# Gated linear attention and a GELU MLP on one core: deeper load buffers, three slots for xT, and more transposes by the DMA crossbar

## The chip, the core and the metric

The kernel runs on one core of one Trainium2 chip. The metric is the device time of one execution in microseconds (us). A core has five engines with instruction streams of their own that meet only at semaphores: TensorE (PE; its weight loads are a row of their own, PEld), VectorE (DVE), ScalarE (ACT), GpSimd (POOL) and SyncE (SP). Sixteen DMA engines move data; here SP and POOL start the transfers.

## What is computed

The first half is a gated recurrent attention over 4 batches, 8 heads, 768 tokens and heads of 48; the second is a two-layer MLP with GELU over all 3072 tokens.

```python
state = zeros((B, H, D, D))                       # B 4, H 8, S 768, D 48
for t in range(S):
    state = alpha[:, :, t, :, None] * state + einsum('bhd,bhe->bhde', k[:, :, t], v[:, :, t])
    y[:, :, t] = einsum('bhd,bhde->bhe', q[:, :, t], state)
x = y.transpose(0, 2, 1, 3).reshape(B * S, H * D)  # 3072 x 384
h = x @ w_in                                       # 384 -> 2048
g = 0.5 * h * (1.0 + tanh(c * (h + 0.044715 * h**3)))
return g @ w_out                                   # 2048 -> 384
```

Inputs and output are float32; the kernel computes in bf16 and f16 with float32 sums.

## The kernel before

**Units and pairs.** The 768 tokens are cut into six chunks `c` of 128. A unit is one chunk of one batch; a *pair* is a chunk of two batches. There are twelve pairs, numbered `m` from 0 to 11: pair 6 and pair 7 are the two pairs of chunk 3, pairs 8 and 9 those of chunk 4, pairs 10 and 11 those of chunk 5. "The seventh pair" is thus pair 6, and "the eighth" pair 7. The two units of a pair are called j = 0 and j = 1 here.

**The steps of one pair.** Loads of alpha (tile `a`), `q`, `k` and v (`vb`) by POOL's DMA queue (L243); the logarithm of alpha on ACT (L296, tile `la`); its running sum as a matmul with a triangle (L313 to L317, tile `cum`); two exponentials on ACT, `b` and `binv` (L342); q' = q * b and k' = k / b on DVE (L353, tiles `qp` and `kp`); both transposed (tile `qkT`); `at` = k' q' for each head on PE (L424, 16 matmuls for the pair); the causal mask on DVE (L431, tile `atm`, four operations); `kv` for the state (L441), which DVE carries on (L463, L466); `y` from the state and from `atm` (L478, L481); `x`, its bf16 copy by ACT or DVE (L488); x transposed (tile `xT`); then the MLP of the pair: 48 matmuls of layer 1 (L507, into `hT`, in eight groups of six), GELU on ACT (L513, eight), and layer 2 (L526, 16 matmuls for each unit into `acc`), the copy `ot` (L538) and the store by SP (L544).

**Two ways to transpose.** On PE, q' and k' of a pair take 16 transposes into PSUM (`turn`, L363) and copies out of it (`turned`, L381); x of a unit takes three transposes (`turn_x`, L495) and one copy by DVE (L499). By the crossbar, SP issues one DMA transpose for q' and one for k' of a pair (`turn_dma`, L401), and one for x of each unit (`turn_x_dma`, L407), straight from SBUF to SBUF. `TURN_QK` and `TURN_X` (L151) list the pairs that go by the crossbar. The DMA queue of SP carries the stores too, in the order in which the program issues them.

**What sets the order.** A list scheduler (`Scheduler.order`, L50) runs when the kernel is built. Each step is a `Task` with a cost for its engine, a priority and what it depends on; buffers are rings with a number of slots (`BUFS`, L158), and a task that takes a slot waits until the users of the slot's last content are done. Loads count as landing one after another. A transpose by the crossbar counts as landed after `W["landed"]`, and later by `late_x` where the caller gives it (L689: `late=W["late_x"] * (m < 7)`). The costs only decide the order; the instructions then run in that order on each engine and wait on the chip for what they need. An instruction of PE that waits keeps all behind it waiting.

**Buffers that the change touches.** `a`, `q`, `k` have 4 slots each, float32 v of the first two pairs (tile `v`) has 2, and bf16 `vb` has 6. `xT` has one tile for each of the six chunks (L194).

Of the kernel before, what the change touches and what calls it, by code (L numbers as in the profile page):

```python
# [5 lines left out]
BF16 = mybir.dt.bfloat16  # L6
F16 = mybir.dt.float16
F32 = mybir.dt.float32
# [128 lines left out]
class _Kernel:  # L137
# [10 lines left out]
             ('a', 1, 0, 1), ('a', 1, 1, 2), ('q', 1, 0, 1), ('k', 1, 0, 1), ('q', 1, 1, 2), ('k', 1, 1, 2))  # L148
    NARROW = (0, 1)

    TURN_QK, TURN_X = (8, 9, 10, 11), (7, 8, 9, 10, 11)  # L151

    EV_ACT = (0, 1, 2, 3)

# [1 line left out]

    URGENT = (2,)
    BUFS = dict(ca=1, yk=2, ff=4, la=3, qp=4, kp=4, b8=2, kn=2, qkT=4, atm=6, x=3, ot=5, bend=3, ends=8,  # L158
                a=4, q=4, k=4, v=2, vb=6)

    def __init__(self, ctx, tc, q, k, v, alpha, w_in, w_out, out):
        nc = self.nc = tc.nc
        self.tc, self.out = tc, out
        B, H, S, D = q.shape
        self.B, self.H, self.S, self.D = B, H, S, D
        C = self.C = 128
        self.NCH = S // C
        self.src = {"a": alpha, "q": q, "k": k, "v": v}
        self.w_in_dram, self.w_out_dram = w_in, w_out
        self.d_model, self.d_ff = w_in.shape  # L170
        self.NKT, self.NFT = self.d_model // C, self.d_ff // C

        self.const = ctx.enter_context(tc.tile_pool(name="const", bufs=1))
        self.sb = ctx.enter_context(tc.tile_pool(name="sb", bufs=1))
        self.ps = ctx.enter_context(tc.tile_pool(name="ps", bufs=1, space=bass.MemoryType.PSUM))

        const = self.const
        self.ut_h = const.tile([C, C], F16, name="ut_h")
        self.ut = const.tile([C, C], BF16, name="ut")
        self.gate = const.tile([C, 1], F32, name="gate")  # L180
        self.ut_blk = [const.tile([C, C], F16, name=f"ut_blk{i}") for i in range(2)]
        self.blk = const.tile([C, 4], F16, name="blk")
        self.ident = const.tile([C, C], BF16, name="ident")
        self.ones = const.tile([C, 1], F16, name="ones")
        self.zero = const.tile([C, 512], BF16, name="zero")
        self.w_in = [const.tile([C, self.NKT, self.d_ff // 4], BF16, name=f"w_in{i}") for i in range(4)]
        self.w_out = const.tile([C, self.NFT, self.d_model], BF16, name="w_out")
        self.half = const.tile([C, 2], F32, name="half")
        self.state = [[const.tile([C, H // 2, 2 * D], BF16, name=f"st{b}_{i}") for i in range(2)]
                      for b in range(B)]  # L190
        self.ring = {n: [const.tile([C, 2, H, 64], F16 if n == "la" else BF16, name=f"{n}{i}")
                         for i in range(self.BUFS[n])] for n in ("la", "qp", "kp")}
        self.used = {n: 0 for n in self.ring}
        self.xT = [const.tile([C, self.NKT, B, C], BF16, name=f"xT{c}") for c in range(self.NCH)]  # L194
        self.NG = 2
        self.gT = [const.tile([C, self.NFT, B * C], BF16, name=f"gT{i}") for i in range(self.NG)]
        self.eng = {"ACT": nc.scalar, "DVE": nc.vector}
# [30 lines left out]
    def load(self, n, c, i, lo=0, hi=2):  # L228

        nc, C, H, D, R = self.nc, self.C, self.H, self.D, self.R  # L230
        u = self.p[c, i]

        def emit(e):
            t = "vb" if n == "v" and u["m"] not in self.NARROW else n
            if t not in u:
                u[t] = self.tile(t, [C, 2, H, D], BF16 if t == "vb" else F32)
            dma = (nc.sync if e == "SP" else nc.gpsimd).dma_start
            src = self.src[n][2 * i + lo:2 * i + hi]
            if u["packed"] and n != "v":
                dma(u[n][:, lo].rearrange("p (o r) d -> p o (r d)", o=2),  # L240
                    src[0, :, c * C:(c + 1) * C].rearrange("h (g r) d -> g h (r d)", r=R))
            else:
                dma(u[t][:, lo:hi].rearrange("t b h d -> t (b h) d"), src.rearrange("b h s d -> s (b h) d")[c * C:(c + 1) * C])  # L243
        return emit
# [159 lines left out]
        return emit  # L404

    def turn_x_dma(self, u, i, c, b):
        return lambda e: self.nc.sync.dma_start_transpose(self.xT[c][:, :, b, :], u["x", i])  # L407

    def attn(self, u, units, apart):
        nc, H, C = self.nc, self.H, self.C  # L410
# [85 lines left out]
        return emit  # L496

    def turned_x(self, u, i, c, b):
        return lambda e: self.copy(e)(self.xT[c][:, :, b, :], u["xT_ps", i])  # L499

    def layer1(self, f, c, lo, hi, nt):
        def emit(e):
            w_in = self.w_in[nt // 4].rearrange("k j (c r) -> k j r c", r=self.NFT // 4)
            h = f["h", c, lo, nt] = self.tile("ff", [self.C, 2, (hi - lo) * self.C], F32, "hT")
            for s in range(2):
                for j in range(self.NKT):
                    self.nc.tensor.matmul(h[:, s], w_in[:, j, nt % 4 + s],  # L507
                                          self.xT[c][:, j, lo:hi].rearrange("p g t -> p (g t)"),
                                          start=j == 0, stop=j == self.NKT - 1, skip_group_check=True)
        return emit  # L510

# [35 lines left out]
    def tasks(self):  # L547
        s = self.s = Scheduler(self.BUFS, self.fill, 60000)
        B, NCH = self.B, self.NCH
# [5 lines left out]
        loads, n, gate, held = {}, 0, [], {}  # L555
# [26 lines left out]
        for step in self.LOADS:  # L582
            if step[0] == "v":
                rows(int(step[1:]), "v")
            elif step[:4] == "gate":
                r, m, j = step[4:].split()
                m, j = int(m), int(j)
# [11 lines left out]
        for m, (c, i) in enumerate(pairs):  # L599
            u, P = self.p[c, i], 100 * m  # L600
# [4 lines left out]
            for lo, hi in self.parts(m):  # L605
# [3 lines left out]
                x = [s.add(e, {"ACT": W[e] if e == "bend" else W["exp"] * n // 2}, P + 2 + j, self.exp(u, e, lo, hi), [cum], LN_EXP)  # L609
                     for j, e in enumerate(("b", "binv", "bend") if u["sums"] else ("b", "binv"))]  # L610
# [35 lines left out]
            vin = [loads["v", m, j] for j in range(2)]  # L646
# [4 lines left out]
            for j in range(2):  # L651
                o, k = P + 10 + 3 * j, kp[j]
# [27 lines left out]
            for j in range(2):  # L680
                b, o, k, ms, turned = 2 * i + j, P + 10 + 3 * j, kp[j], masks[j], turns[j]
                at = ats[m][-1 if m not in self.SINGLE else j]
                if m in self.NARROW:
                    vin[j].deps += turned
                y = s.add("y", {"PE": W["intra"] + (W["inter"] if c else 0)}, P + 20 + j, self.y(u, j, c, b),
                          ms + turned + [vin[j]] + ([states[b, c - 1]] if c else []))
                xc = s.add("x", {"ACT": W["xc_act"], "DVE": W["xc"]}, P + 20 + j, self.x(u, j), [y])
                if m in self.TURN_X:
                    xe = tx = s.add("turn", {"SP": W["turn"]}, P + 22 + j, self.turn_x_dma(u, j, c, b), [xc], xbar=W["xbar_x"], late=W["late_x"] * (m < 7))  # L689
                else:  # L690
                    tx = s.add("tx", {"PE": W["tx"]}, P + 22 + j, self.turn_x(u, j), [xc])
                    xe = s.add("xe", {"DVE": W["xe"]}, P + 22 + j, self.turned_x(u, j, c, b), [tx])
                    tx.take("yk", xe)
                y.take("yk", xc)
                xc.take("x", tx)
                users += [at, y]
                ms[0].take("atm", y)
                xts[c, b], ys[b, c] = xe, y
                vs.append(y)
                if c < NCH - 1:  # L700
                    if u["packed"]:
                        tb = s.add("t", {"PE": W["t4"]}, P + 29 + j, self.turn_back(u, j), turned)
                        k = s.add("ev", {"DVE": W["ev4"], "ACT": W["ev4_act"]}, P + 29 + j, self.turned_back(u, j), [tb])
                        tb.take("yk", k)
                        users.append(tb)
                        backs.append(tb)
                    kv = s.add("kv", {"PE": W["kv"]}, P + 30 + j, self.kv(u, j), [k, vin[j]])
                    st = states[b, c] = s.add("st", {"DVE": W["st" if c else "st0"]}, P + 30 + j, self.carry(u, j, c, b),
                                              [kv, end] + ([states[b, c - 1], ys[b, c - 1]] if c else []))
                    kv.take("yk", st)  # L710
                    vs.append(kv)
                    kvs.append(kv)
                    cs.append(st)
# [9 lines left out]
            qp[0].take("qp", *tq)  # L723
            kp[0].take("kp", *tq, *kvs)
            if m in self.NARROW:
                loads["v", m, 0].take("v", *vin)
                vin[0].take("vb", *vs)
            else:
                loads["v", m, 0].take("vb", *vs)
# [6 lines left out]
        f, gs, l2s, ots, parts_of, firsts = {}, {}, {}, [], [], []  # L736
# [108 lines left out]
```

## Time and profile before

| what | value |
|---|---|
| median of the runs | 181.47 us (181.79, 180.89, 183.69, 181.16) |
| the profiled execution | 181.33 us |
| its span in the profile | 179.6 us |
| granted TensorE clock | 1.00 |
| busy: DVE / ACT / POOL | 96.8 / 130.9 / 57.8 us |
| DMA moved | 28.14 MB, mean 157 GB/s |
| crossbar transposes | 10 of x, 4 of q', 4 of k' |
| chain that ended last, by engine | PE 90%, DMA 5%, ACT 1%, DVE 1% |

The profile is one execution, taken by the hardware profiler; times in it run from the span's start. A timeline line gives the start, the length, the engine, the line of the kernel, the operation with output<-input, the shape and the number of instructions merged. A row of a table by stretches gives the stretch, its length, then the busy time of PE, PEld, DVE, ACT and POOL with the number of instructions in brackets, the granted clock, the mean share of the DMA engines (above 1 when packets queue on an engine) and GB/s. A DMA row ends with the median time from issue to landing.

### The profile page before, as it was taken

What the parts mean: (1) busy time and instruction counts of PE and PEld (TensorE: products, weight loads), DVE (VectorE), ACT (ScalarE), POOL (GpSimd) and SP (SyncE); (2) the same over time, 40 slices, a digit from 0 to 9 for tenths busy, and PEclk for the clock granted to TensorE, in tenths of its full rate; (3) what the DMA queues carried; (4) which work ended last, traced back from release to release, by engine and by line L of the source; (5) the groups of instructions that cost most, each with busy time, mean ns of one, the idle gap of its engine ahead of it and who ended that gap; (6) DMA issues with size and microseconds to landing.
All of it is one profiled execution on the core that took longest, in us unless ns stands there. A gap on an engine that the chain in (4) does not pass through costs nothing.

```text
span 179.6 us, 4459 instructions
## 1 busy us (share of the span) xinstructions
PE 173.1 (96%) x1860; PEld 136.7 (76%) x1860; DVE 96.8 (54%) x191; ACT 130.9 (73%) x216; POOL 57.8 (32%) x64
## 2 busy tenths in 40 slices
PE   6979999999999999999999999999999999999993
PEld 2557699566896897798698779689688697796972
DVE  6579750145968795597499798199245415000000
ACT  4669778974898678858888757887987984491831
POOL 2396447984647766722721300000000000000000
PEclk9999999999999999999999999999999999999999
DMA  4999999999999999998992626552361270311102
GB/s 126 270 275 198 209 241 238 240 214 206 223 306 189 223 252 206 197 261 197 181 248 67 169 98 108 102 131 55 68 161 47 61 183 10 90 41 47 44 0 88
DMA packets 45956, 28.14 MB, mean 157 GB/s; under 512 B 34544, under 2 KB 42352, under 8 KB 45936
## 3 DMA queue, kind: packets, MB, share of 16 engines
q0 software_dynamic: 26464, 17.70, 59.1%
q1 hardware_dynamic: 19472, 10.16, 21.4%
q8 instruction: 14, 0.23, 0.6%
q14 instruction: 6, 0.05, 0.1%
HBM read 25.17 MB, written 4.72 MB: 166 GB/s over the span
## 4 chain that ended last, share of the span: by engine, by line
PE 90%; DMA 5%; ACT 1%; DVE 1%; SPq 0%; issue 0%; POOL 0%
PE hT L507 35%; PE acc L526 35%; PE at L424 4%; DMA v<-in_v_dram 3%; PE qkT_ps L363 3%; PE yps L481 3%; PE kv L441 2%; PE cum L313 2%; PE yps L478 2%; DMA a<-in_alpha_dram 2%; PE xT_ps L495 1%; PE idle L224 1%; PE cum L281 1%; PE cum L315 1%; PE k_ps L389 1%; ACT vb L324 1%
## 5 line engine op out<-in xcount | busy, mean ns | idle before, releaser
L507 PE MATMUL hT<-xT,w_in 128*128 128x256 bf16 x576 | 69.2, 273 | 0.0
L526 PE MATMUL acc<-w_out,gT 128*128 128x384 bf16 (+1 forms) x400 | 69.1, 319 | 0.0
L513 ACT ACTIVATE gT<-hT 128x512 bf16<-128x512 f32 x96 | 56.7, 597 | 16.5 <-PE hT L507 12.9
L507 PEld LDWEIGHTS <-w_in 128*128 128x128 bf16 x576 | 61.0, 113 | 1.2
L526 PEld LDWEIGHTS <-gT 128*128 128x128 bf16 x400 | 36.7, 97 | 19.2
L431 DVE TENSOR_TENSOR atm<-at,ut 128x512 bf16<-128x512 f32 x48 | 30.3, 683 | 13.2 <-PE at L424 13.1
L353 DVE TENSOR_TENSOR qp<-q,b 128x768 bf16<-128x768 f32 (+1 forms) x15 | 11.9, 794 | 25.3 <-ACT b L342 25.3
L538 ACT COPY ot<-acc 128x384 f32<-128x384 f32 (+1 forms) x18 | 8.3, 458 | 14.1 <-PE acc L526 11.9
L243 POOL DMA_DIRECT2D q<-in_q_dram x11 | 12.2, 1110 | 15.5 <-DVE xT L499 7.4
L243 POOL DMA_DIRECT2D vb<-in_v_dram x11 | 12.1, 1102 | 10.6 <-PE xT_ps L495 6.1
L243 POOL DMA_DIRECT2D k<-in_k_dram x11 | 12.2, 1107 | 4.9 <-DMA a<-in_alpha_dram 1.8
L243 POOL DMA_DIRECT2D a<-in_alpha_dram x11 | 12.2, 1114 | 4.5 <-DMA w_in<-in_moe_w_in_dram 1.4
L342 ACT ACTIVATE b<-cum 128x768 bf16<-128x768 f32 (+1 forms) x15 | 10.3, 683 | 3.9 <-PE cum L315 2.5
L215 ACT ACT_TABLE_LOAD x9 | 11.5, 1283 | 0.9 <-PEq L829 0.7
L353 DVE TENSOR_TENSOR kp<-k,binv 128x768 bf16<-128x768 f32 (+1 forms) x15 | 11.9, 791 | 0.0
L513 ACT ACT_TABLE_LOAD x9 | 11.5, 1283 | 0.2
L342 ACT ACTIVATE binv<-cum 128x768 bf16<-128x768 f32 (+1 forms) x15 | 10.2, 680 | 0.0
L381 DVE COPY qkT<-qkT_ps 128x1024 bf16<-128x1024 bf16 (+1 forms) x13 | 8.6, 686 | 2.7 <-PE qkT_ps L363 2.6
L488 DVE CAST x<-yps 128x384 bf16<-128x384 f32 x11 | 6.1, 558 | 7.0 <-PE yps L481 6.9
L224 PE MATMUL idle<-zero 128*128 128x512 bf16 x26 | 8.5, 436 | 1.2 <-DVE half L798 1.2
L463 DVE TENSOR_TENSOR stmp<-kv,st 128x384 f32<-128x384 f32 x16 | 8.8, 552 | 1.2 <-PE kv L441 1.2
L488 ACT CAST x<-yps 128x384 bf16<-128x384 f32 x13 | 6.2, 475 | 4.4 <-PE yps L481 4.4
(63 smaller groups left out, 165.8 us busy)
## 6 DMA issues: line engine op xcount, KB each, us to landing
out_dram<-ot SPq DMA_DIRECT2D x23, 192.0 KB, 2.3
a<-in_alpha_dram POOLq DMA_DIRECT2D x9, 384.0 KB, 11.4
q<-in_q_dram POOLq DMA_DIRECT2D x9, 384.0 KB, 11.2
k<-in_k_dram POOLq DMA_DIRECT2D x9, 384.0 KB, 11.3
vb<-in_v_dram POOLq DMA_DIRECT2D x9, 192.0 KB, 11.2
w_in<-in_moe_w_in_dram POOLq DMA_DIRECT2D x4, 384.0 KB, 9.6
w_out<-in_moe_w_out_dram POOLq DMA_DIRECT2D x4, 384.0 KB, 11.2
a<-in_alpha_dram SPq DMA_DIRECT2D x4, 192.0 KB, 4.0
```

Of the source, the lines that this page charges most:

```text
L215: nc.scalar.add_instruction(mybir.InstLoadActFuncSet(name=nc.get_next_instruction_name(), act_func_set_id=i, engine=mybir.EngineType.Activ ...
L224: self.nc.tensor.matmul(ps, self.zero[:, 0:self.C], self.zero, start=True, stop=True)
L243: dma(u[t][:, lo:hi].rearrange("t b h d -> t (b h) d"), src.rearrange("b h s d -> s (b h) d")[c * C:(c + 1) * C])
L342: self.nc.scalar.activation(u[n].rearrange("t i h d -> t i (h d)")[:, lo:hi], cum, AF.Exp, scale=1.0 if n == "b" else -1.0)
L353: self.nc.vector.tensor_tensor(out, rows, b, op=ALU.mult)
L381: self.copy(e)(t, ps)
L431: self.nc.vector.tensor_tensor(u["atm", i][:, o], u["at", i][o], self.ut[:, None, :].to_broadcast([self.C, self.H // 2, self.C]), op=ALU.mult)
L463: nc.vector.tensor_tensor(s, acc, old, op=ALU.add)
L488: self.copy(e)(x, u["y", i].rearrange("t h d -> t (h d)"))
L507: self.nc.tensor.matmul(h[:, s], w_in[:, j, nt % 4 + s], self.xT[c][:, j, lo:hi].rearrange("p g t -> p (g t)"), start=j == 0, stop=j == se ...
L513: return lambda e: self.nc.scalar.activation(self.gT[c % self.NG][:, nt:nt + 2, lo * self.C:hi * self.C], f.pop(("h", c, lo, nt)), AF.Gelu ...
L526: self.nc.tensor.matmul(f["acc", c, b][:, lo:hi], self.gT[c % self.NG][:, nt, b * self.C:(b + 1) * self.C], self.w_out[:, nt, lo:hi], star ...
```

## The change

Pair 7 is added to the pairs whose q' and k' are transposed by the crossbar, and pair 6 to those whose x is; `late_x` is counted for pairs below 6 instead of below 7. `a` gets 6 slots, `q` and `k` 5; the float32 v of pairs 0 and 1 takes slots of the ring of `a` and its own ring goes. `xT` has three tiles, which the chunks use in turn.

```diff
-    TURN_QK, TURN_X = (8, 9, 10, 11), (7, 8, 9, 10, 11)
+    TURN_QK, TURN_X = (7, 8, 9, 10, 11), (6, 7, 8, 9, 10, 11)
...
-                a=4, q=4, k=4, v=2, vb=6)
+                a=6, q=5, k=5, vb=6)
...
-        self.xT = [const.tile([C, self.NKT, B, C], BF16, name=f"xT{c}") for c in range(self.NCH)]
+        self.NX = 3
+        self.xT = [const.tile([C, self.NKT, B, C], BF16, name=f"xT{c}") for c in range(self.NX)]
...
-                u[t] = self.tile(t, [C, 2, H, D], BF16 if t == "vb" else F32)
+                u[t] = self.tile("a" if t == "v" else t, [C, 2, H, D], BF16 if t == "vb" else F32, t)
...
-        return lambda e: self.nc.sync.dma_start_transpose(self.xT[c][:, :, b, :], u["x", i])
+        return lambda e: self.nc.sync.dma_start_transpose(self.xT[c % self.NX][:, :, b, :], u["x", i])
...
-        return lambda e: self.copy(e)(self.xT[c][:, :, b, :], u["xT_ps", i])
+        return lambda e: self.copy(e)(self.xT[c % self.NX][:, :, b, :], u["xT_ps", i])
...
-                                          self.xT[c][:, j, lo:hi].rearrange("p g t -> p (g t)"),
+                                          self.xT[c % self.NX][:, j, lo:hi].rearrange("p g t -> p (g t)"),
...
-                    xe = tx = s.add("turn", ..., xbar=W["xbar_x"], late=W["late_x"] * (m < 7))
+                    xe = tx = s.add("turn", ..., xbar=W["xbar_x"], late=W["late_x"] * (m < 6))
...
-                loads["v", m, 0].take("v", *vin)
+                loads["v", m, 0].take("a", *vin)
```

What the scheduler makes of it: PE's order is the same up to the `y` of pair 6; there its six transposes of x and the 16 of q' and k' of pair 7 are gone. Behind that point PE now does 12 matmuls of layer 2, `kv` of pair 6, 4 more of layer 2, `cum` of pair 8, 16 of layer 2, the first six of layer 1 of pair 6, `at` and `kv` of pair 7, 30 of layer 1, `at` of pair 8, and `y` of pairs 7 and 8 with layer 1 and layer 2 between. From `at` of pair 10 on, the order is as before. DVE loses two copies of `qkT` and two of `xT`. SP gains four transposes and has ten stores ahead of its first transpose, not twelve; its order there is x of pair 6 (j = 0), q' of pair 7, x of pair 6 (j = 1), k' of pair 7, a store, q' and k' of pair 8, a store, x of pairs 7 and 8. POOL's loads are the same up to v of pair 5; behind it those of `a`, `q` and `k` stand further ahead: the load of `vb` for pair 11 now stands behind all of `a` and all but the last `q` and `k`, where before two of `a`, two of `q` and two of `k` came after it.

More of the change, by code (lines that the diff above doesn't have):

```diff
@@ L688, in tasks @@
                 if m in self.TURN_X:
-                    xe = tx = s.add("turn", {"SP": W["turn"]}, P + 22 + j, self.turn_x_dma(u, j, c, b), [xc], xbar=W["xbar_x"], late=W["late_x"] * (m < 7))
+                    xe = tx = s.add("turn", {"SP": W["turn"]}, P + 22 + j, self.turn_x_dma(u, j, c, b), [xc], xbar=W["xbar_x"], late=W["late_x"] * (m < 6))
                 else:
```

## The prediction

> **What bounds the kernel now.** I read the engine shares first, then the table by stretches, to see whether the bound is the same where the change lies.
>
> ```profile
> PE 173.1 (96%) x1860; PEld 136.7 (76%) x1860; DVE 96.8 (54%) x191; ACT 130.9 (73%) x216; POOL 57.8 (32%) x64
> ```
> ```profile
> 60.00:97.00 37.00, 37.00 (x440) 30.91 (x439) 27.65 (x52) 28.20 (x43) 18.38 (x17) 1.00 1.25 213
> 97.00:130.00 33.00, 33.00 (x387) 26.13 (x385) 23.19 (x42) 26.40 (x42) 2.30 (x2) 1.00 0.46 99
> 130.00:160.90 30.90, 30.90 (x302) 25.39 (x301) 10.04 (x15) 23.29 (x36) 0.00 (x0) 1.00 0.33 86
> ```
>
> From 60 to 160.9 us PE has no idle time at all, at full clock; DVE and ACT have room. The chain that ended last is 90% PE. So a matmul taken off PE in this part shortens the kernel by its slot, provided PE then waits for nothing. The removed work is in the next lines (start, length, what): x of pair 6, and q' and k' of pair 7.
>
> ```profile
> 97.44 0.33 PE L495 MATMUL xT_ps<-ident,x 128*128 128x128 bf16 x3
> 97.61 1.46 PE L526 MATMUL acc<-w_out,gT 128*128 128x384 bf16 x8
> 98.91 0.33 PE L495 MATMUL xT_ps<-ident,x 128*128 128x128 bf16 x3
> 99.07 0.81 PE L526 MATMUL acc<-w_out,gT 128*128 128x384 bf16 x4
> 99.72 0.39 PE L363 MATMUL qkT_ps<-ident,qp 128*128 128x128 bf16 x4
> 99.95 0.39 PE L363 MATMUL qkT_ps<-ident,kp 128*128 128x128 bf16 x4
> 100.17 0.39 PE L363 MATMUL qkT_ps<-ident,qp 128*128 128x128 bf16 x4
> 100.39 0.39 PE L363 MATMUL qkT_ps<-ident,kp 128*128 128x128 bf16 x4
> 100.62 0.33 PE L313 MATMUL cum<-la,ut_h 128*128 128x384 f16 x1
> ```
>
> The lengths overlap in PE's pipeline; what counts is start to next start: 0.17 us for three (97.44 to 97.61), 0.22 for four, 0.90 for sixteen (99.72 to 100.62).
>
> **Part 1, PE.** Removed: 2 x 0.17 = 0.34 us for x and 0.90 us for q' and k', together **1.24 us**. All else on PE is moved, with its number unchanged. The same five groups of `at` are each followed by something else than `at` as before, so the 0.12 us that the next group takes longer there (0.78 for six matmuls of layer 1 after `at`, 0.66 elsewhere, in the chain of waits) appears as often.
>
> [...]
>
> **Part 2, DVE.** Two `qkT` copies (0.64 us each) and two `xT` copies (0.36) go, 2.0 us of a DVE that has 9.8 us free between 97 and 130. Taken at nothing; its cover is that idle time, and it brings k' of pair 7 forward (98.08 to 97.7, with no copy in between).
>
> **Part 3, loads.** POOL waits for a slot twice late in the kernel:
>
> ```profile
> 84.18 1.15 POOL L243 DMA_DIRECT2D vb<-in_v_dram  x1 [6.07 <-PE xT_ps L495]
> ...
> 98.18 1.15 POOL L243 DMA_DIRECT2D q<-in_q_dram  x1 [7.07 <-DVE xT L499]
> ```
> ```profile
> 96.00:98.00 2.00, 2.00 (x30) 1.86 (x28) 1.93 (x4) 1.88 (x4) 0.00 (x0) 1.00 0.00 0
> 98.00:100.00 2.00, 2.00 (x19) 1.35 (x18) 1.47 (x4) 1.97 (x3) 1.71 (x2) 1.00 0.00 0
> 100.00:102.00 2.00, 2.00 (x33) 1.61 (x31) 1.63 (x3) 1.07 (x2) 0.58 (x1) 1.00 0.94 247
> ```
>
> The DMA runs dry from 96 to 100 us, and the last q and k land only at 99.43 + 5.0 = 104.4. With the new slots, `a` of pairs 10 and 11 and q, k of pair 10 go out in the 6 us that POOL now waits before 84.18, and the last q and k follow the q' and k' of pair 6 (DVE, 87.45 to 89.2). Between 82 and 88 the DMA moved 193, 114 and 144 GB/s in stretches of 2 us where it moves about 260 when fed: 0.66 MB of room, against 0.79 MB for that last q and k. So all loads end at about 96 us (0.13 MB more at 250 GB/s, 0.5 us, behind what ends at 95.6 now). No load is late for PE before or after: PE never waits from 60 on. Cost 0; its worth is an empty DMA for part 4.
>
> **Part 4, the new waits.** PE is in order: if the first six of layer 1 of pair 6 wait for its x, or `at` of pair 7 for k', everything behind waits. The nearest row is the chain that is the first by the crossbar now, of the same four transposes:
>
> ```profile
> 107.24 1.27 SPq L407 DMA_TRANSPOSE xT<-x  x1
> 108.62 1.24 SPq L401 DMA_TRANSPOSE qkT<-qp  x1
> 109.96 1.21 SPq L407 DMA_TRANSPOSE xT<-x  x1
> 111.27 2.24 SPq L401 DMA_TRANSPOSE qkT<-kp  x1
> ```
>
> Each holds SP's queue for about 1.3 us; from issue to landing these four took 2.4, 3.3, 4.1 and 3.6 us; in later chains 2.3 to 3.0. In the changed kernel: x (j = 0) of pair 6 is written by DVE until 95.85 and issued at 95.9; q' (written to 97.77) at 97.8; x (j = 1, ACT, to 98.23) when SP is free, at 99.1; k' (98.65) at 100.4. Landed: x at 101.5 to 103.2, k' at 103.1 to 104.0. No store stands in front: the next `ot` is ready at about 100.9, behind k'.
>
> PE meanwhile, from 97.44: 12 of layer 2 (0.1625 each) to 99.39, `kv` 0.34, 4 of layer 2 to 100.38. Then `cum` of pair 8 needs `la`, which ACT ends at 99.55 + 0.84 = 100.39; with the semaphore a wait of about **0.1 us**. `cum` 0.53, 16 of layer 2 2.60: layer 1 of pair 6 is due at 103.6 and `at` of pair 7 at 104.3. Margins: 0.4 to 2.1 us for x, 0.3 to 1.2 us for k'. Next, q' and k' of pair 8: the exponentials start 0.7 after `cum` (101.2), DVE is done with q' at 102.95 and k' at 103.9; SP, behind k' of pair 7 and one store, issues them at 103.3 and 104.7; k' lands at 107.4 to 108.3, due at 108.6 (104.3 + 0.55 + 0.45 + 3.28). Margin 0.3 to 1.2. Then `y` of pair 8 needs two masks (0.62 each) behind the state's four operations (2.2 us from 107.4): 110.8, due at 111.3. I take 0 for these three, the upper end being the slowest landings seen. The upper bound of a crossbar landing next to full load traffic is the nearest row of that state, stores: between 40 and 50 us they took
>
> ```profile
> out_dram<-ot SPq DMA_DIRECT2D x4, 192.0 KB, 7.8
> ```
>
> against 1.9 to 2.3 with the loads gone: 5.8 us more. Below nothing: no wait of PE exists here that could go, so no further gain.
>
> Three slots of `xT` cost nothing: chunk 3 writes over chunk 0, whose layer 1 is long past, with its four results stored between 40 and 50 us.
>
> **Sum.** 181.33 (profiled; span 179.6 and 1.73 around it) - 1.24 + 0.1 = **180.2 us**, 0.6% below its own time and 0.7% below the median 181.47.
>
> **Rivals.** What a measurement of this kernel can tell from no change is about 0.5%, 0.9 us.
>
> A, *the gain turns into a wait*: PE stands at the first layer 1 of pair 6, at `at` of pair 7 or of pair 8, since margins are 0.3 us at their lower end. For it: these are the kernel's earliest crossbar transposes, and the first chain of before had the slowest landings. Against: those landings still fit. One landing 0.7 to 1.5 us later than the slowest row gives a wait of 0.4 to 1.2: 180.6 to 181.4; with half of the 5.8 us above, k' of pair 7 lands at 100.4 + 2.8 + 2.9 = 106.1, a wait of 1.8, and the time is 182.0, still within 0.5%. The form in which the change doesn't do what it says belongs here: if PE's slots were really set by GELU (ACT needs 0.64 us for each, PE 0.66 for the six matmuls that feed it), the freed 1.24 us would be idle and the time stay at 181.3; ACT's 6.6 us of idle time between 97 and 130 speaks against it.
>
> B, *slower*: the loads, let ahead by more slots, still fill the DMA engines when the transposes start, and PE waits at `at` of pair 7. Price: k' lands at 100.4 + 2.8 + 5.8 = 109.0, due at 104.3, a wait of 4.7: 180.2 + 4.7 = 184.9. It decides from a wait of 1.24 - 0.1 + 0.9 = 2.0 us on, that is, if loads run past 100 us instead of ending at 96. For it: the last loads end just where the first transpose starts. Against: x (j = 0), which meets them, has 7 us of room, and only 0.79 MB has to move forward.
>
> **How the numbers follow.** Forecast 180.2 with its own bounds 179.7 to 180.55: 0.52. A: 0.31. B: 0.17. The forecast's chance is that of faster by over 0.5%, A's that of within 0.5%, B's that of slower. The range should leave out no more than 2 in 10: it takes the forecast's bounds, with 0.1 below them, and all of A, and leaves out B: 179.6 to 182.0.
>
> **What would show it.** Right: 22 matmuls fewer on PE; PE idle below 0.3 us from 97 to 160; POOL's waits of 6.07 and 7.07 smaller or gone, no load issued after 91; the first crossbar transpose at about 96, k' of pair 7 landed before 104.2. Wrong: a wait of PE or PEld at L507 or L424 ended by a DMA; landings above 4 us between 96 and 109; load traffic after 98; DVE's masks of pair 8 late and PE idle at L481; or a place earlier than 97 us at which PE now waits for a load or a store made late by the denser traffic.

## The result, and the profile after

| | median of the runs | profiled execution | its span |
|---|---|---|---|
| before | 181.38 us (70 runs) | 181.33 | 179.6 |
| after | 181.09 us (46 runs) | 181.18 | 179.4 |

The ratio after / before is 0.9986, 95% interval 0.9978 to 0.9994: 0.25 us faster, where 1.1 us were forecast. The time lies in the stated range, but most of the forecast gain is missing. Lines of the changed kernel have numbers one higher than those of before.

The table by stretches, same columns as before:

```profile
60.00:97.00 37.00, 37.00 (x442) 30.96 (x441) 27.66 (x51) 28.39 (x43) 21.09 (x19) 1.00 1.40 228
97.00:130.00 33.00, 32.09 (x365) 24.85 (x363) 21.66 (x38) 26.98 (x42) 0.00 (x0) 1.00 0.48 100
130.00:160.90 30.90, 30.90 (x302) 25.39 (x301) 9.66 (x15) 23.24 (x37) 0.00 (x0) 1.00 0.33 88
```

One cell has changed in kind: PE is busy 32.09 of 33.00 us between 97 and 130, where it had no idle time. The missing 0.91 us is one wait. PE's timeline, and the chain that ended last around it (start, length, what):

```profile
103.38 0.82 PE L508 MATMUL hT<-xT,w_in 128*128 128x256 bf16 x6
105.11 0.62 PE L425 MATMUL at<-qkT 64*128 64x128 bf16 x16 [0.91 <-DMA qkT<-kp]
105.66 0.52 PE L442 MATMUL kv<-vb,kp 128*128 128x96 bf16 x8
```
```profile
100.28 4.79 DMA qkT<-kp
105.06 0.05 issue
105.11 0.62 PE at L425 x16
```

`at` of pair 7 could start at 104.20 and starts at 105.11, when k' has landed. (Behind the same six matmuls, where nothing waits, `at` starts 0.75 us after their start, in the run with halves below for one; here it starts 1.73 us after it. So the wait costs 0.98 us of PE's time.) SP's queue shows that k' was issued in time (predicted 100.4), and the row of its landing how long it was under way:

```profile
100.28 1.26 SPq L402 DMA_TRANSPOSE qkT<-kp  x1
101.63 0.53 SPq L545 DMA_DIRECT2D out_dram<-ot  x1
```
```profile
qkT<-kp SPq DMA_TRANSPOSE x1, 4.8
```

4.8 us, against 2.7 or 2.8 for the other k' transposes that meet nothing. What held it is in the table by half microseconds (the last two columns are DMA share and GB/s):

```profile
102.50:103.00 0.50, 0.50 (x5) 0.30 (x4) 0.50 (x2) 0.48 (x2) 0.00 (x0) 1.00 3.53 75
103.00:103.50 0.50, 0.50 (x6) 0.32 (x4) 0.50 (x1) 0.50 (x1) 0.00 (x0) 1.00 0.00 0
103.50:104.00 0.50, 0.50 (x7) 0.44 (x4) 0.50 (x2) 0.35 (x1) 0.00 (x0) 1.00 0.06 6
104.00:104.50 0.50, 0.20 (x2) 0.00 (x0) 0.23 (x2) 0.26 (x1) 0.00 (x0) 1.00 0.18 44
104.50:105.00 0.50, 0.00 (x0) 0.00 (x0) 0.00 (x0) 0.34 (x1) 0.00 (x0) 1.00 1.04 358
```

From 103 to 104.5 the DMA moves 0 to 44 GB/s, and a share of 3.53 in the half before says that packets begun there stayed open for long: the share counts a packet's whole time where it starts. The trace's single packets show which. One 256-byte packet of k' and 13 packets of the store behind it are open from about 102.5 to 104.5, and in that time the instruction queue fetches one 16 KB block:

```
after, open packets of SP's queue   102.44 to 104.43  (256 bytes, k')
                                    102.66 to 104.47  (1536 bytes, store)  and 12 more like it
after, packet of instruction queue  102.71 to 103.67  (16 KB)
before, k' of pair 8                open 112.94 to 113.79; fetch 111.77 to 112.97 (16 KB)
before, q' and x of pairs 8 and 7   open 110.26 to 110.93; fetch 109.57 to 110.17 (8 KB)
```

The page of either kernel counts the 16 KB packets, 14 in a run:

```profile
q8 instruction: 14, 0.23, 0.6%
```

From one to the next 184 to 281 PE instructions start in the kernel after (248 in the mean, weight loads counted), so they are taken here for the fetches of PE's instruction stream; the records do not say whose they are. The runs below that add PE instructions move them. Whose the 8 KB block is, the profile does not say. The slow landings of before, from which the prediction took its upper ends, had such neighbours.

The rest went as forecast: POOL's waits of 6.07 and 7.07 us are gone, and the last load is issued at 89.77.

```profile
88.63 1.15 POOL L244 DMA_DIRECT2D q<-in_q_dram  x1 [1.50 <-DVE qp L354]
89.77 1.15 POOL L244 DMA_DIRECT2D k<-in_k_dram  x1
```

### The profile page after: what moved, and what is told of

The parts are those of the page before. It is cut to its first block, busy times and chain, and to the rows that moved or that the text cites. A ratio compares the mean times of both kernels' runs of the same rounds, so it can differ in the third digit from the quotient of the medians.

```text
span 179.4 us, 4421 instructions
## 1 busy us (share of the span) xinstructions
PE 172.0 (96%) x1838; PEld 135.3 (75%) x1838; DVE 95.1 (53%) x187; ACT 131.4 (73%) x216; POOL 57.9 (32%) x64
## 4 chain that ended last, share of the span: by engine, by line
PE 87%; DMA 8%; ACT 1%; DVE 1%; SPq 0%; issue 0%; POOL 0%
PE hT L508 35%; PE acc L527 33%; PE at L425 4%; DMA v<-in_v_dram 3%; PE qkT_ps L364 3%; DMA qkT<-kp 3%; PE yps L482 3%; PE kv L442 2%; PE yps L479 2%; PE cum L314 2%; DMA a<-in_alpha_dram 2%; PE xT_ps L496 1%; PE idle L225 1%; PE cum L282 1%; PE cum L316 1%; PE k_ps L390 1%
## 5 line engine op out<-in xcount | busy, mean ns | idle before, releaser
L467 DVE TENSOR_TENSOR st<-stmp,ends 128x384 bf16<-128x384 f32 x16 | 8.9, 558 | 0.6
```

Of the source, the lines that this page charges most:

```text
L467: nc.vector.tensor_tensor(new.rearrange("f p (o d) -> f (p o) d", o=2), acc.rearrange("f p (o d) -> f (p o) d", o=2), ends, op=ALU.mult)
```

## The experiments

Three theories for k' being late: **F**, the fetch of PE's instructions holds a crossbar transpose until after the fetch has ended; **S**, the store issued 1.35 us behind k' does; **L**, load traffic does. Single profiles differ at the start (the first `y` of pair 6 comes between 94.39 and 95.91 us), so besides the time each run is read by a stretch of its profile: from the first `y` of pair 6 to the start of the last layer 2.

| run | median us | ratio to before (95%) | stretch | fetch at | k' pair 7: issue, landing after | PE waits there |
|---|---|---|---|---|---|---|
| before | 181.4 | 1 | 76.46 | | by PE | |
| after | 181.09 | 0.9986 (0.9978 to 0.9994) | 76.23 | 102.71 to 103.67 | 100.3, 4.8 | 0.91 |
| after, again | 181.17 | 0.9978 (0.9961 to 0.9995) | 75.65 | 102.19 to 103.21 | 100.3, 4.2 | 0.33 |
| 64 instructions | 181.17 | 0.9983 (0.9968 to 0.9998) | 75.26 | 101.48 to 102.47 | 101.6, 3.5 | 0 |
| no store | 180.84 | 0.9972 (0.9956 to 0.9989) | 75.74 | 101.93 to 102.96 | 100.1, 4.3 | 0.41 |
| old buffers | 186.90 | 1.0309 (1.0284 to 1.0334) | 81.90 | 105.69 to 107.01 | 100.7, 8.1 | 2.26 and 1.84 |
| `at` later | 180.65 | 0.9961 (0.9943 to 0.9978) | 75.50 | 103.06 to 104.68 | 100.7, 2.8 | 0 |
| halves | 180.50 | 0.9967 (0.9945 to 0.9990) | 75.26 | 100.83 to 101.79 | 100.9, 3.6 | 0 |
| halves, `at` later | 180.87 | 0.9958 (0.9930 to 0.9987) | 75.51 | 100.01 to 100.94 | 100.2, 3.4 | 0 |
| buffers only | 181.41 | 1.0010 (0.9995 to 1.0024) | 76.45 | | by PE | |
| before, halves | 182.22 | 1.0059 (1.0038 to 1.0080) | 76.88 | 134.23 to 135.24 | (pair 10) 132.2, 4.2 | 0.37 |
| 8 halves | 181.23 | 0.9986 (0.9968 to 1.0003) | 75.52 | 101.97 to 103.32 | 100.9, 4.1 | 0.20 |
| quarters | 180.54 | 0.9941 (0.9923 to 0.9960) | 75.25 | 96.89 to 97.97 | 100.5, 2.8 | 0 |

**64 instructions** more at the start of PE's stream (`pad` is 36 in the first fill, which gives up four of its own matmuls, and 0 in the others):

```diff
+            for _ in range(pad):
+                self.nc.tensor.matmul(ps[:, 0:16], self.zero[:, 0:self.C], self.zero[:, 0:16], start=True, stop=True)
-            for _ in range(n):
+            for _ in range(n - pad // 9):
```

> Edit: 32 more matmuls net (64 PE instructions with their weight loads) stand in front of the first fill matmuls, in time that PE fills anyway; nothing else changes. In the profile of the changed kernel PE waits 0.91 us at `at` of pair 7 for k', which lands 4.8 us after its issue; a 16 KB packet of the instruction queue (one comes about every 256 PE instructions) moves from 102.7 to 103.7 us, and all packets of the crossbar queue are stuck until 104.4. Theory F (the fetch of PE's instructions holds the transposes): the fetches come 64 PE instructions earlier in the order of the work, the one in question at about 99.3 us, before k' is issued at 100.3; k' lands 2.7 to 3.0 us after its issue, PE's wait goes, and the time falls by 0.9 us to about 180.2 (ratio to before 0.993 to 0.995). Theory S (the store that SP issues 1.35 us behind k' slows it) and theory L (load traffic does): nothing they depend on changes, so the wait stays at 0.9 and the time at 181.1 (ratio 0.998 to 0.999).

PE's wait is gone and the stretch 0.97 us shorter than after, as F says; the fetch came to 101.48, not 99.3, and k' still landed in 3.5. q' of the same chain now met the fetch, and took 4.5. The time does not show the gain. The profiled execution (181.59) reached pair 6 1.4 us later than the profile after (95.91 for 94.54), so that in it the start took back what the wait gave; whether by the 36 matmuls or by the loads there is open, and so is whether the other executions did the same.

**No store** behind k' (the tile of chunk 2, batch 2 is not written):

```diff
+        if (c, b) == (2, 2):
+            return lambda e: None
         return lambda e: self.nc.sync.dma_start(self.out[r:r + self.C, sl], f["ot", c, b][:, sl])
```

> Edit: one store is left out, the one that SP issues right behind k' of pair 7 (the result tile of chunk 2, batch 2 is not written to memory). Theory S: k' lands 2.8 us after its issue, PE's wait of 0.91 us goes, about 180.2 (ratio 0.993 to 0.995). Theory F: the PE instruction fetch still falls into k', the wait stays at 0.7 to 1.0 us and the time at 181.0 (ratio 0.997 to 0.999). Theory L: as F.

S falls: with no store there, k' still takes 4.3 us and PE waits 0.41. The fetch came 0.8 us earlier in this run, and k' landed 0.6 earlier.

**Old buffers**, with the transposes kept:

```diff
-                a=6, q=5, k=5, vb=6)
+                a=4, q=4, k=4, v=2, vb=6)
```

> Edit: the changed kernel with the load buffers of before (a, q, k of 4 slots, v of 2); the transposes of pair 6 and pair 7 stay on the crossbar, xT stays in three slots, and PE's order is that of the changed kernel. The last q and k loads then go out at about 98 and 99 us and run to 103 or 104, beside the four transposes. Theory L: the landings of x and q', k' get longer than in the changed kernel by up to the 5 us that stores showed under load; PE waits 2 to 5 us at layer 1 of pair 6 or at `at` of pair 7; 182 to 185 us (ratio 1.005 to 1.02). Theory F: k' is held by the fetch until 104.4 as before; the loads add at most 1 us; 181 to 182 (ratio 0.998 to 1.004).

Slower by about 5.5 us, and above the 182 to 185 that L forecast. The last q and k go out at 98.38 and 99.52, x (j = 1) of pair 6 lands after 6.8 us and k' of pair 7 after 8.1. PE's timeline of this run:

```profile
102.79 1.14 PE L527 MATMUL acc<-w_out,gT 128*128 128x384 bf16 x6
106.19 0.82 PE L508 MATMUL hT<-xT,w_in 128*128 128x256 bf16 x6 [2.26 <-DMA xT<-x]
108.84 1.04 PE L425 MATMUL at<-qkT 64*128 64x128 bf16 x16 [1.84 <-DMA qkT<-kp]
```

This is what rival B forecast: beside the loads this x and k' took 6.8 and 8.1 us, against 2.3 and 4.8 in the kernel after, whose new buffers bring the last load to an end at 99.4. x lands at 106.14, just behind the last packet of the loads (105.97). The second wait is not the loads' alone: a fetch (105.69 to 107.01) falls into k' here too, and packets of k' stay open until 107.8. Without the buffers the change costs about 5.5 us. It does not say what holds k' in the kernel after, where the loads have ended.

**`at` of pair 7 later**: `late=800 * (m == 7)` for the tasks of q' and k', by which PE does `kv` of pair 7 and one group of layer 1 first.

> Edit: the scheduler counts q' and k' of pair 7 as landed 800 ns later; it moves `kv` of pair 7's predecessor work and one group of layer 1 (0.34 + 0.66 = 1.0 us of PE work) ahead of `at` of pair 7. Theories F, S and L alike: `at` of pair 7 stands 1.0 us later, k' lands at about 105.0 as it does now, the wait of 0.91 shrinks to 0.0 to 0.2 us, time 180.2 to 180.5 (ratio 0.993 to 0.996), unless the masks of pair 7, 1 us later than now, make `y` of pairs 7 or 8 wait: then up to 181.1.

There is no wait for k', and 0.7 us of the stretch's 1.0 are seen in the time (180.65, a little above the forecast). But this profile does not show what the run was for: k' landed after 2.8 us, not at 105.0. Its packets were through at 103.0, just before the fetch (103.06), and it is the store and q' of pair 8 behind it that landed late instead (after 4.0 and 3.8 us). PE was done with the six matmuls in front of the old place of `at` at about 104.5, and k' had landed at 103.5, so in this execution `at` would not have waited at its old place either. That the later place covers a late landing in the other executions is not shown. The stretch stays 0.25 us above that of the next run; 0.09 of it is a wait at 107.69 that a mask by DVE ended, the rest is open.

**Halves**: every fill as two matmuls of 256 columns, 52 instructions more in the same time.

```diff
-                self.nc.tensor.matmul(ps, self.zero[:, 0:self.C], self.zero, start=True, stop=True)
+                for w in range(2):
+                    self.nc.tensor.matmul(ps[:, 256 * w:256 * w + 256], self.zero[:, 0:self.C], self.zero[:, 0:256], start=True, stop=True)
```

> Edit: each of the 26 fill matmuls of 512 columns is written as two of 256; the same columns, 52 PE instructions more (with the weight loads), all in stretches that PE fills anyway, so that the start costs nothing, unlike in the run with 64 small instructions, whose first crossbar transpose came 1.4 us later. Theory F (the fetch of PE's instructions holds a crossbar transpose until after its end): the fetch of 102.7 us comes at about 100 us; k' of pair 7 lands 2.8 to 3.2 us after its issue, PE does not wait at `at` of pair 7, time 180.2 (ratio 0.993 to 0.995). Theory L (load traffic alone makes k' late): the wait stays, 181.1 (ratio 0.998 to 0.999).

PE's timeline has no wait, and the 33 us are full:

```profile
103.97 0.82 PE L509 MATMUL hT<-xT,w_in 128*128 128x256 bf16 x6
104.72 0.62 PE L426 MATMUL at<-qkT 64*128 64x128 bf16 x16
```
```profile
97.00:130.00 33.00, 33.00 (x372) 25.63 (x371) 22.61 (x39) 27.92 (x43) 0.00 (x0) 1.00 0.42 100
```

The fetch now falls on q' (4.6 us) and x; k', issued just as it starts, lands after 3.6 and in time. The stretch is 1.20 us below before, the forecast's 1.24 nearly whole. L without F falls: the loads are those of the kernel after. The median is 180.5, 0.3 above F's forecast and 0.86 below before, which is a ratio of 0.9953; the recorded ratio of the runs is 0.9967, and its interval holds both.

**Halves and `at` later** together:

> Edit: both the fills in two halves and `at` of pair 7 one group of layer 1 and `kv` later. Theory F: the wait is gone by either, together no more than by the first: 180.2 (ratio 0.993 to 0.995). If something else still holds PE after `at` of pair 7 (0.25 us of the late version's gain were missing), it is 180.4 to 180.7.

No more than by one, as expected, and the 0.25 us of the later `at` stay. The median, 180.87, lies above both forecasts.

**Buffers only**, with the transposes of before:

> Edit: the new load buffers and the three slots of xT, with the transposes of before (x from pair 7, q' and k' from pair 8 by the crossbar). All theories: PE waited for no load before, so 181.2 to 181.6 (ratio 0.999 to 1.001); the last load is issued before 91 us and lands before 99. If the denser load traffic cost PE something on its own, it is slower here by that.

Nothing gained and nothing lost: the buffers alone are worth 0, and are the condition for the rest.

**The kernel before, with halves**, meant as a control:

> Edit: the kernel before, with its fills written as two halves. A control: there PE waits for no crossbar transpose, so a shift of the instruction fetches by 52 instructions changes nothing: 181.4 (ratio 0.998 to 1.002). If the halves themselves save or cost time at the start, it shows here.

The control fails, in a way that tells more than its success would have. The start costs nothing (the first `y` of pair 6 comes at 94.68, in before at 94.72). But here the shift brings a fetch, 134.23 to 135.24, onto k' of pair 10, which lands 4.2 us after its issue instead of 2.7, and a kernel that had no such wait gets one:

```profile
136.51 0.62 PE L425 MATMUL at<-qkT 64*128 64x128 bf16 x16 [0.37 <-DMA qkT<-kp]
```

Of the 0.86 us by which the median rose the profile shows 0.4 in the stretch; that execution was the fastest of the seven (181.85), so the others may have waited longer; not shown.

**The change again**:

> The changed kernel once more, beside the next two on one chip. 181.1 (ratio 0.997 to 0.999); in its profile the fetch of about 102.7 us and k' of pair 7 landing 4 to 5 us after its issue, PE waiting 0.5 to 1.0 us there; from `y` of pair 6 to the start of the last layer 2, 76.2 us (76.46 before, 75.26 with the fills in halves).

The time is as forecast; the wait and the stretch (75.65) are below it. The same kernel waits 0.33 us in this profile and 0.91 in the first: the fetch came 0.5 us earlier.

**Eight halves**, 16 instructions:

> Edit: only the first 8 fills are halved, 16 PE instructions more. Theory F: the fetch comes about 0.6 us earlier than in the changed kernel and k' lands as much earlier (about 1.4 us after the fetch's end); the wait is 0.2 to 0.5 us, and the stretch from `y` of pair 6 to the last layer 2 takes 75.5 to 75.9 us; time 180.6 to 180.9 (ratio 0.995 to 0.998). If the wait did not come from the fetch but from anything that halving changes in kind, it would be all or nothing: 76.2 or 75.26.

The time misses the forecast: 181.23, with an interval that holds 1. The profile is as F has it, a wait of 0.20 between nothing and all.

**Quarters**, 156 instructions:

```diff
-                self.nc.tensor.matmul(ps, self.zero[:, 0:self.C], self.zero, start=True, stop=True)
+                for w in range(4):
+                    self.nc.tensor.matmul(ps[:, 128 * w:128 * w + 128], self.zero[:, 0:self.C], self.zero[:, 0:128], start=True, stop=True)
```

> Edit: all 26 fills in quarters, 156 PE instructions more than the changed kernel. Theory F: fetches at about 95, 108, 118, 129 and 144 us, none on k' of pair 7 (issued at 100.3) or of pair 8 (104.2); the one at 144 falls on k' of pair 11, which would land 0.5 to 1 us late, at or just before its due time. The stretch takes 75.2 to 75.6 us; time 180.2 to 180.6 (ratio 0.993 to 0.996), plus what four weight loads for each fill cost at the start, if any.

A second position, and again no wait:

```profile
104.08 0.62 PE L426 MATMUL at<-qkT 64*128 64x128 bf16 x16
```
```profile
qkT<-kp SPq DMA_TRANSPOSE x1, 2.8
```

The fetch falls at 96.89, between x and q' of the first chain. The later fetches came elsewhere than forecast, at 140.34 for one instead of 144: there x of pair 10 was held (4.2 us), and k' of pair 11 landed in 2.8. At 180.54 against 181.52 of before on the same chip, a ratio of 0.9941, this version has the lowest ratio of all, and beats both kernels.

## Why the prediction was wrong, point by point

- **What bounds it, and part 1.** Right. With no wait the stretch is 1.20 us shorter (halves) and 1.21 (quarters), against 1.24 forecast. No wait but the one for k' is new in PE; `y` of pair 8 did not wait for its masks.
- **Part 2, DVE.** Right: with the four copies gone no wait of PE for DVE went or came.
- **Part 3, loads.** The mechanism was right, its time not: the last k landed at 89.77 + 9.6 = 99.4 us, not at 96. The DMA moved 191 to 213 GB/s between 84 and 90, not 260. What it cost was landings of 4.2 and 3.1 us for x (j = 0) and q', which had room. The run with the old buffers, whose last k lands at 99.52 + 8.6 = 108.1, shows what a longer overlap would have cost.
- **Part 4, the new waits: the step that failed.** Issue and due times were right within 0.2 us (k' issued at 100.28, due at 104.20; `cum` did not wait the 0.1 us). "I take 0 for these three, the upper end being the slowest landings seen" is the step: k' took 4.8 us and landed at 105.1, not at 103.1 to 104.0, and PE waited 0.91 us where the sum has 0. The 3.3, 4.1 and 3.6 us in the rows of before were taken as the slow end of a spread, and I did not ask what made three of four transposes with no loads beside them slower than the later ones. The trace of before has two instruction fetches beside them (109.57 to 110.17 and 111.77 to 112.97). (The fourth of the SP rows shown is also misread: it holds SP for 2.24 us, not about 1.3. And one landing in the later chains took 3.1 us, not 3.0 at most.) In these runs k' of pair 7 took 3.4 to 3.6 us where the fetch began up to 0.2 us ahead of its issue, 4.1 to 4.3 where it began 1.0 to 1.9 us behind it, and 4.8 or 2.8 where it began 2.4 us behind it, so that the 3.6 us of one such row were no upper end for the next.
- **Rival A** is what came, in its first form: one landing later than the slowest row of k' by 1.2 us, at a place named, with a time (181.09) inside the 180.6 to 181.4 given for it. Its cause, the fetch, was not named at all; "the kernel's earliest crossbar transposes" was not it, for in the runs with halves and quarters these are as early and PE does not wait.
- **Rival B** was excluded by the buffers, as argued, and its price (184.9) was too low: the old buffers gave 186.9. The waits were 4.1 us, near the 4.7 it had; PE's clock, which fell as well, was not in the sum.

## What to carry to other kernels

A slow row among equal ones was not a spread here: find its neighbour in time before using it as an upper end. When work moves from a busy engine to a transfer, its margin has to cover the slowest landing seen beside what else the DMA moves there, instruction fetches included, and the 1.1 us that k' had here beyond a landing of 2.8 were no margin: the longest hold in these traces, with the loads gone, was 2.1 us (q' of pair 8 in the kernel before with halves, 4.8 for 2.7). Kernels with the same work and another number of instructions in the fills differed here by 0.86 us (before, without and with halves) and by 0.63 (the change again, and quarters); their profiles show 0.4 us of either in the stretch where the slower one waits for a k' that landed beside a fetch. So a change of the instruction count in idle time is worth a run.

## What the runs showed of the hardware

- The 14 packets of 16 KB of the instruction queue took 0.88 to 1.52 us each in the kernel after, 184 to 281 PE instructions apart, and came at other places of the work in the runs that add instructions ahead (table above). Crossbar packets under way, and a store behind them, then stayed open until about 0.8 us after the packet's end (after 103.67 to 104.43; before 112.97 to 113.79, and with the 8 KB block 110.17 to 110.93).
- Counted packet by packet: k' is 1024 packets of 256 bytes, of which 111 to 114 began in each 0.1 us from 101.7 to 102.1 in the first profile of the kernel after, 7 for each of the sixteen DMA engines if they share evenly (an estimate), and 106, 106 and 103 in the next three steps. 31 were left, which began one after another from 103.66 to 104.45, the first of them within 0.02 us of the fetch's end (103.67). In the second run of that kernel 112 began from 102.1 to 102.2, in which the fetch starts (102.19), and 105 and 106 in the two steps behind it; the first of the rest began at 103.19, for a fetch that ends at 103.21. In the kernel before with halves these times are 135.23 and 135.24. What was missing in these steps, 6 and 7 packets in the second run, is about one engine's share; but the records do not name the engine, and why those packets waited is not shown. In the first profile the share is missing from 102.05 on, 0.7 us before the fetch's packet is recorded.
- In the 13 traces together, behind the last load, the 62 transposes of x without an instruction fetch (8 or 16 KB) between issue and landing took 2.3 to 2.4 us, the 77 with one 2.3 to 4.3; k' took 2.7 to 3.0 without (44) and 2.7 to 4.8 with (17).
- A store landed late beside a fetch too. In the kernel after, the one issued at 163.63, with no transpose near it, met the fetch of 164.38 to 165.73 and landed after 3.4 us; the stores around it took 1.8 to 1.9. Of loads no such delay is shown: no packet of a load was open for longer than 0.54 us between 33 and 88 us of the profile after, where five such blocks were fetched, but that late store had no packet open for longer than 0.2 us either.
- In the run with the old buffers the granted clock fell from 1.00 to 0.50 behind PE's gap of 2.26 us:

```profile
104.00:106.00 2.00, 0.00 (x0) 0.00 (x0) 0.61 (x3) 0.23 (x1) 0.00 (x0) 1.00 1.17 196
106.00:108.00 2.00, 0.82 (x6) 0.55 (x5) 0.00 (x0) 0.60 (x1) 0.00 (x0) 0.74 1.32 46
108.00:110.00 2.00, 1.16 (x19) 0.96 (x20) 0.51 (x1) 0.00 (x0) 0.00 (x0) 0.50 1.22 311
...
112.00:114.00 2.00, 2.00 (x12) 1.48 (x11) 1.93 (x4) 1.15 (x2) 0.00 (x0) 0.56 0.00 0
```

  The 0.74 from 106 to 108 puts the fall at about 106.95, an estimate that takes it for one step from 1.00 to 0.50. That is 3.0 us after PE fell idle (102.79 + 1.14 = 103.93), with PE back at work for about 0.8 us since 106.19, and before the gap of 1.84 us began (107.00). So by this estimate the second gap is not its cause. By the 0.56 from 112 to 114 the clock was at 0.50 until about 113.8, by the same kind of estimate, and it was at 1.00 after 114. The two waits are 4.1 us; the stretch grew by 5.7 over that of the kernel after, which has 0.91 of wait itself, so about 2.5 us are left. An estimate of the clock's part fits: PE worked from 108.84 to 113.8 at half the clock, which loses half of 4.9 us. Beside the waits of 0.91, 0.41 and 0.37 us (the kernel after, no store, before with halves) the row of the stretch has 1.00. What sets the clock is not shown; the run has one gap of 2.26 us, and a fall about 0.8 us after PE was back at work.
